# Expert outputs sent one by one to DRAM, with accumulating DMAs, in a fused retention and mixture-of-experts kernel

## The chip, the cores and the metric

The kernel runs on one core of a Trainium2 chip. A core has a matrix engine (TensorE, PE in the profile, with its weight loads as PEld), a vector engine (VectorE, DVE), a scalar engine (ScalarE, ACT), GpSimd (POOL) and SyncE (SP), which issues most DMAs. The metric is the device time of one execution in microseconds (us), the median of several runs. Less is better.

## The reference

The first stage is a causal retention over 8 batches, 8 heads, 576 positions and 64 values per head. The second is a mixture of 4 experts, whose outputs are weighted by normalised probabilities and summed:

```python
scores = scale * np.matmul(q, k.transpose(0, 1, 3, 2))
Dmat = np.where(rel >= 0, gamma[:, None, None] ** rel[None, :, :], 0.0)
attn = np.matmul(scores * Dmat[None], v)              # 8 x 8 x 576 x 64
x = attn.transpose(0, 2, 1, 3).reshape(4608, 512)
p = domain_probs / (domain_probs.sum(-1, keepdims=True) + 1e-09)
for e in range(4):                                    # w1[e] 512 x 1024, w2[e] 1024 x 512
    h = np.maximum(x @ w1[e], 0.0)
    out += p[:, e:e + 1] * (h @ w2[e])                # out 4608 x 512, float32
```

## The kernel before

The 4608 tokens are cut into 9 tiles of 512 (`nt` 0 to 8), and a tile into 4 subtiles of 128 tokens. A stage is one tile and one expert. All weights stay in SBUF as bf16.

Tile 0 and the up projection of tile 1's expert 0 are done in a head with ordinary matmuls, while attention of the batches 0 and 1 runs. After it come the stages from tile 1, expert 1 on. In each, `up_fast` computes the up projection of the stage with one level of a Strassen-like scheme (seven products for eight) in two halves, g = 0 and g = 1. Between its products it calls `fill(1)` to `fill(4)`, which put matmuls of the previous stage's down projection in between, so that TensorE has work while the other engines move results. From a certain stage on for each expert the down projection uses the scheme too (class `Down`, one object per half, with banks V and W in PSUM): half `s` of a stage yields the subtiles `s` and `s + 2`. For tile 1's experts 0 and 3 and tile 2's expert 0, as for tile 0, it is the ordinary one (`downs`, which yields the subtiles 0 to 3 in order).

The work of attention for the batches 2 to 7 stands in queues of one class (`Chain`), one queue per engine. Every call of `between`, `window` and `sums` takes the next piece whose needs were emitted before. The order of the instructions on each engine is thus fixed when the program is built, and each engine runs its own in order.

Rows of the program that the steps below touch:

- L684: VectorE adds P and m5 into bank R (`upR`). The next product of TensorE into P waits until it has read P.
- L692 and L693: VectorE adds, then GpSimd applies the ReLU to that quarter of hT.
- L593, L595, L597, L599: VectorE makes the sums of hT that the next `Down` needs. L593 of half 1 stands between the two outputs (`last_sum`).
- L569 to L572: VectorE makes the token sums of the next tile, when a tile begins.
- L650, L652, L654: `Down.out`. For expert 0, VectorE scales the output from V (L652) and ScalarE the one from W (L650) into `acc`. For experts 1 to 3, VectorE does both as one fused scale and add on `acc` (L654).
- L529 and L531: the same for the ordinary path, scaled by ScalarE for expert 0 and added by VectorE for the others.
- L657 and L534: after expert 3, SP sends the finished subtile of 256 KB to DRAM.
- L333 and L339 to L340: the masks of attention on VectorE, and on ScalarE with an affine select on GpSimd. L242: ScalarE copies attention's output into the tile of tokens. L279 to L291: GpSimd casts raw loads. L366 and L369: running sums of attention's state. L297 and L299: SP issues DMA transposes. L111 to L133: SP issues the raw loads, each when a cast has set a raw buffer free. L420: the casts of batch 0 on VectorE and GpSimd. L148 and L153: GpSimd issues the weight loads, which cast float32 to bf16.
- L672 and L623: the matmuls of the up and of the down projection.

The accumulators lie in SBUF: four buffers of 128 x 512 float32, one for each subtile of a tile, kept over the tile's four experts.

Of the kernel before, what the change touches and what calls it, by code (L numbers as in the profile page):

```python
# [9 lines left out]
FP32 = mybir.dt.float32  # L10
# [4 lines left out]
MULT = mybir.AluOpType.mult  # L15
ADD = mybir.AluOpType.add
# [7 lines left out]
def kernel(  # L24
# [10 lines left out]
    nc = tc.nc  # L35
    B, H, S, D = q.shape
    N, E = moe_domain_probs.shape
    _, Dm, F = moe_w1.shape
# [8 lines left out]
    NFC = F // 128  # L47
    NT = 512
    n_nt = N // NT
    NSUB = NT // 128  # L50
# [8 lines left out]
    att1 = ctx.enter_context(tc.tile_pool(name="att1", bufs=1))  # L59
    att2 = ctx.enter_context(tc.tile_pool(name="att2", bufs=2))  # L60
    hpool = ctx.enter_context(tc.tile_pool(name="hpool", bufs=2))
    apool = ctx.enter_context(tc.tile_pool(name="apool", bufs=NSUB))
    xpool = ctx.enter_context(tc.tile_pool(name="xpool", bufs=3))
    tpool = ctx.enter_context(tc.tile_pool(name="tpool", bufs=1))
    psum = ctx.enter_context(tc.tile_pool(name="psum", bufs=1, space=PSUM))
# [6 lines left out]
    def bank(ring, shape, dtype, name):  # L72
        tag = RINGS[ring][turn[ring] % len(RINGS[ring])]
        turn[ring] += 1
        return psum.tile(shape, dtype, tag=tag, name=name)
# [4 lines left out]
    def after(ins, dep):  # L80
        tc.add_manual_dep(ins.ins, dep.ins.name,
                          mybir.DependencyInfo(mybir.DependencyClass.Sync, mybir.DependencyReason.DATA),
                          reason="start order")
# [58 lines left out]
    w1_sb, w2_sb = [], []  # L142
# [71 lines left out]
    probs = const.tile([128, E, NTT], FP32)  # L214
# [36 lines left out]
    class Att:  # L251


        def __init__(self, b):
            self.b, self.t = b, state[b]
            self.m, self.qkT, self.sT, self.s = {}, {}, {}, {}
# [235 lines left out]
                put_x(nc.vector, slice(2 * u, 2 * u + 2), self.b * S + 256 * hf + c * C, os[c])  # L492


    acc, hTs, tsum, ssum, dsum, hsum = {}, {}, {}, {}, {}, {}

    def up_classical(nt, e, lead=0, cut=NT // 2, pause=False):
# [21 lines left out]
    def downs(nt, e, ring):  # L519

        hT = hTs[nt, e]
        if e == 0:
            acc[nt] = [apool.tile([128, Dm], FP32, tag="acc", name="acc") for _ in range(NSUB)]

        def evacuate(po, ns, cols):
            t = nt * NSUB + ns
            pe, a = probs[:, e, t:t + 1], acc[nt][ns][:, cols]
            if e == 0:
                nc.scalar.activation(a, po, Copy, scale=pe)  # L529
            else:  # L530
                nc.vector.scalar_tensor_tensor(a, po, pe, a, op0=MULT, op1=ADD)  # L531
            if e == E - 1:
                eng = nc.scalar if cols.start else nc.sync
                eng.dma_start(out=out[t * 128:(t + 1) * 128, cols], in_=a)  # L534

        for ns in range(NSUB):
            w = Dm // 2 if (nt, ns, e) == (n_nt - 1, NSUB - 1, E - 1) else Dm
            for d in range(0, Dm, w):
                po = bank(ring, [128, w], FP32, "po")
                for fc in range(NFC):  # L540
                    nc.tensor.matmul(po, lhsT=hT[:, fc, ns * 128:(ns + 1) * 128],  # L541
                                     rhs=w2_sb[e][:, fc, d:d + w], start=(fc == 0), stop=(fc == NFC - 1))
                    yield None if fc < NFC - 1 else lambda: evacuate(po, ns, slice(d, d + w))

    def down_groups(nt, e):
        for f in downs(nt, e, "mm"):
            if f:
                f()
                yield
# [51 lines left out]
    class Down:  # L601
# [2 lines left out]

        def __init__(self, nt, e, s, tags=("o0", "o1")):
            self.nt, self.e, self.s, self.tags = nt, e, s, tags
            if e == 0 and s == 0:
                acc[nt] = [apool.tile([128, Dm], FP32, tag="acc", name="acc") for _ in range(NSUB)]

        def product(self, i, part=slice(0, NFC // 2)):  # L610
            hT, h, w, t = hTs[self.nt, self.e], hsum[self.nt, self.e], w2_sb[self.e], dsum[self.e]
# [28 lines left out]
            nc.vector.tensor_tensor(o, i, x, op=ADD)  # L640

        def out(self, i, halves=(slice(0, 2),)):
            ns = 2 * i + self.s
            t, po = self.nt * NSUB + ns, (self.V, self.W)[i]
            pe = probs[:, self.e, t:t + 1]
            for x in halves:
                cols = slice(x.start * HD, x.stop * HD)
                a, src = acc[self.nt][ns][:, cols], po[:, x].rearrange("p a d -> p (a d)")
                if self.e == 0 and i == 1:
                    nc.scalar.activation(a, src, Copy, scale=pe)  # L650
                elif self.e == 0:
                    nc.vector.tensor_scalar_mul(a, src, pe)  # L652
                else:
                    nc.vector.scalar_tensor_tensor(a, src, pe, a, op0=MULT, op1=ADD)  # L654
                if self.e == E - 1:
                    eng = nc.scalar if len(halves) == 1 and x.start else nc.sync
                    eng.dma_start(out=out[t * 128:(t + 1) * 128, cols], in_=a)  # L657

    def up_fast(nt, e, g, fill, window, sums):

# [334 lines left out]
    for nt, e in [(nt, e) for nt in range(1, n_nt) for e in range(E)][1:]:  # L995
        fast = before >= begin[before[1]]
        fill_classical = None if fast else downs(*before, "po")
        while pay(nt, e, late=True):
            pass
# [142 lines left out]
```

## Time and profile before

| what | value |
|---|---|
| median of 3 runs | 521.08 us (520.82 to 521.61) |
| the profiled execution's own time | 521.82 us |
| its span, first to last instruction | 520.1 us |
| HBM read, written | 45.16 MB, 9.44 MB |
| output DMAs | 32 of 256 KB and 8 of 128 KB, all issued by SP |
| VectorE, L654 | 88 of 512 columns, 0.749 us (from V) and 0.742 us (from W) |
| ScalarE, L650 | 12, 0.689 us |
| VectorE, L652 | 12, 0.751 us |

The profile is of one execution. "Busy" is the time in which an engine executes; a row of the timeline has the start, the length, engine, line, operation, the tiles written and read, and, in brackets, how long the engine was idle before it and what released it. Releasers are inferred from semaphores. A matmul's start tells more than its end, which is modelled.

### The profile page before, as it was taken

Reading aid. Unit: us, or ns where it says so; the run is one execution under the profiler, and the core shown is the slowest. Engines: PE = TensorE matmul, PEld = TensorE weight load, DVE = VectorE, ACT = ScalarE, POOL = GpSimd, SP = SyncE. Lnnn points to the kernel's source line nnn. Section 1 sums busy time; section 2 is a strip of 40 time slices with the busy share of each in tenths; the row PEclk is TensorE's granted clock in tenths of the full one; section 3 lists DMA queues with packets and bytes.
Section 4 is the critical chain, followed back from the end, with each engine's and each line's share of the span. In section 5 each row is a group of like instructions: output and inputs, shape, how many; then the busy total and the mean of one; then the engine's idle time right before and its main releaser. Section 6 shows DMA issues by size and latency. Waiting matters only on the chain.

```text
span 520.1 us, 12551 instructions
## 1 busy us (share of the span) xinstructions
PE 505.5 (97%) x4871; PEld 401.6 (77%) x4886; DVE 388.8 (75%) x720; ACT 308.7 (59%) x637; POOL 196.1 (38%) x299
## 2 busy tenths in 40 slices
PE   8999999999999999999999999999999999999995
PEld 3644455678667878888888888888888888888884
DVE  6624579877646888779877987887788878787776
ACT  3462264666446756666666666766666667666661
POOL 6702275644433444444443543354345310000010
PEclk9999999999999999999999999999999999999999
DMA  9999998926183145525463538433941020011002
GB/s 239 187 208 201 199 204 184 160 48 113 42 203 62 42 101 134 137 57 114 95 159 72 112 70 196 72 89 65 204 95 42 13 80 2 2 41 42 2 1 82
DMA packets 149836, 54.24 MB, mean 104 GB/s; under 512 B 131308, under 2 KB 144620, under 8 KB 149776
## 3 DMA queue, kind: packets, MB, share of 16 engines
q1 hardware_dynamic: 142448, 45.05, 40.1%
q0 software_dynamic: 7328, 8.39, 9.5%
q8 instruction: 38, 0.62, 0.5%
q14 instruction: 22, 0.18, 0.1%
HBM read 45.16 MB, written 9.44 MB: 105 GB/s over the span
## 4 chain that ended last, share of the span: by engine, by line
PE 89%; DVE 7%; issue 2%; DMA 1%; ACT 0%; DVEq 0%; SPq 0%
PE upP L672 20%; PE downV L623 18%; PE downW L623 13%; PE upR L672 10%; PE po L541 8%; PE ph L500 6%; PE upQ L672 5%; PE s L328 2%; DVE acc L654 1%; PE oc L379 1%; PE kvp L346 1%; DVE upR L684 1%; PE oc L376 1%; DMA raw<-in_q_dram 1%; DVE sT L333 1%
## 5 line engine op out<-in xcount | busy, mean ns | idle before, releaser
L672 PEld LDWEIGHTS <-wt 128*128 128x128 bf16 x992 | 94.9, 98 | 18.0 <-issue 3.8
L623 PEld LDWEIGHTS <-hT 128*128 128x128 bf16 x928 | 90.8, 98 | 11.1 <-issue 0.6
L693 POOL TENSOR_SCALAR hT<-hT 128x512 bf16<-128x512 bf16 x62 | 38.3, 618 | 160.5 <-DVE hT L692 160.4
L672 PEld LDWEIGHTS <-wsum 128*128 128x128 bf16 x744 | 72.7, 98 | 12.2 <-issue 2.6
L623 PE MATMUL downV<-wt,hT 128*128 128x256 bf16 x464 | 78.4, 273 | 0.4 <-DVE acc L654 0.4
L672 PE MATMUL upP<-xT,wt 128*128 128x256 bf16 x496 | 74.4, 272 | 2.1 <-DVE upR L684 1.7
L623 PEld LDWEIGHTS <-hsum 128*128 128x128 bf16 x696 | 67.8, 98 | 8.7 <-DVE hsum L593 0.3
L684 DVE TENSOR_TENSOR upR<-upP,m 128x512 f32<-128x512 f32 x62 | 43.1, 696 | 35.8 <-PE upP L672 22.1
L700 ACT ACTIVATE hT<-upP 128x512 bf16<-128x512 f32 x62 | 37.0, 597 | 53.0 <-PE upP L672 39.2
L695 ACT ACTIVATE hT<-upR 128x512 bf16<-128x512 f32 x62 | 37.0, 597 | 32.7 <-PE upR L672 32.6
L541 PE MATMUL po<-wt,hT 128*128 128x512 bf16 x214 | 52.1, 379 | 0.6
L678 ACT ACTIVATE upQ<-upP 128x512 f32<-128x512 f32 x62 | 36.3, 586 | 26.0 <-PE upP L672 25.9
L340 POOL TENSOR_SCALAR_AFFINE_SELECT sT<-sT 128x512 bf16<-128x512 bf16 x24 | 15.2, 634 | 96.1 <-ACT sT L339 80.4
L654 DVE SCALAR_TENSOR_TENSOR acc<-downV,probs,acc 128x512 f32<-128x512 f32 (+1 forms) x48 | 34.6, 726 | 22.5 <-PE downV L623 22.4
L686 ACT ACTIVATE hT<-upQ 128x512 bf16<-128x512 f32 x62 | 37.0, 597 | 22.3 <-PE upQ L672 22.3
L692 DVE TENSOR_TENSOR hT<-upP,m 128x512 bf16<-128x512 f32 x62 | 42.8, 690 | 6.5 <-PE upP L672 4.7
L516 ACT ACTIVATE hT<-ph 128x512 bf16<-128x512 f32 x40 | 23.5, 597 | 29.1 <-PE ph L500 28.2
L672 PE MATMUL upR<-tsum,wsum 128*128 128x256 bf16 x248 | 37.2, 272 | 2.3 <-DVE tsum L569 2.3
L680 ACT ACTIVATE m<-upR 128x512 f32<-128x512 f32 x62 | 36.8, 594 | 2.2 <-PE upR L672 2.2
L672 PE MATMUL upP<-tsum,wt 128*128 128x256 bf16 x248 | 37.3, 273 | 0.1
L672 PE MATMUL upP<-tsum,wsum 128*128 128x256 bf16 x248 | 37.2, 273 | 0.0
L672 PE MATMUL upR<-xT,wsum 128*128 128x256 bf16 x248 | 37.2, 273 | 0.0
(136 smaller groups left out, 974.2 us busy)
## 6 DMA issues: line engine op xcount, KB each, us to landing
out_dram<-acc SPq DMA_DIRECT2D x32, 256.0 KB, 2.9
wt<-in_moe_w_dram POOLq DMA_DIRECT2D x6, 1024.0 KB, 26.2
raw_k<-in_k_dram SPq DMA_DIRECT2D x24, 256.0 KB, 3.3
raw_q<-in_q_dram SPq DMA_DIRECT2D x24, 256.0 KB, 3.6
raw_v<-in_v_dram SPq DMA_DIRECT2D x24, 256.0 KB, 3.8
raw<-in_k_dram SPq DMA_DIRECT2D x8, 256.0 KB, 5.6
raw<-in_q_dram SPq DMA_DIRECT2D x8, 256.0 KB, 5.8
raw<-in_v_dram SPq DMA_DIRECT2D x8, 256.0 KB, 5.5
```

The source lines that it names most:

```text
L541: nc.tensor.matmul(po, lhsT=hT[:, fc, ns * 128:(ns + 1) * 128], rhs=w2_sb[e][:, fc, d:d + w], start=(fc == 0), stop=(fc == NFC - 1))
L623: nc.tensor.matmul(o, lhsT=l[:, k, self.s * 128:(self.s + 1) * 128], rhs=r[:, k], start=(i == 1 and k == 0), stop=(k == NFC // 2 - 1), ski ...
L654: nc.vector.scalar_tensor_tensor(a, src, pe, a, op0=MULT, op1=ADD)
L672: nc.tensor.matmul(ps[:, l], lhsT=wa(kc)[:, f:f + 128], rhs=xa(kc), start=(start and l == 0 and kc == 0), stop=(kc == 1), skip_group_check ...
L678: nc.scalar.activation(Q, P, Copy)
L680: nc.scalar.activation(m5, R_, Copy)
L684: nc.vector.tensor_tensor(R_, P, m5, op=ADD)
L686: nc.scalar.activation(hT[:, lo, t0], Q, Relu)
L692: nc.vector.tensor_tensor(h22, P, m5, op=ADD)
L693: nc.gpsimd.tensor_scalar(h22, h22, float("inf"), 0.0, op0=MIN, op1=MAX)
L695: nc.scalar.activation(hT[:, lo, t1], R_, Relu)
L700: nc.scalar.activation(hT[:, hi, t0], P, Relu)
```

## The change

In tiles 1 to 7 nothing is accumulated in SBUF any more. Each expert's output is scaled by its probability into a buffer of two subtiles: the first of a pair by VectorE and the second by ScalarE on the path of `Down`, both by ScalarE on the ordinary path. Then the pair (512 KB) is sent. For expert 0, SP sends it as a plain write. For experts 1 to 3, GpSimd issues a DMA that adds to what is in DRAM. Such a DMA waits for the landing of those that wrote the same rows for the expert before. The pairs are (s, s + 2) on the path of `Down`, and (0, 1) and (2, 3) on the ordinary one. Tiles 0 and 8 go on adding in SBUF and are sent after expert 3. The buffers are two of 128 x 2 x 512 in place of four of 128 x 512. The ordinary path loses its splitting of the very last output in two halves.

```diff
-    apool = ctx.enter_context(tc.tile_pool(name="apool", bufs=NSUB))
+    apool = ctx.enter_context(tc.tile_pool(name="apool", bufs=2))
...
+    out_rows = out.rearrange("(x p) d -> p x d", p=128)
+    sent = {}
+
+    def on_chip(nt):
+        return nt in (0, n_nt - 1)
+
+    def out_pair(nt, e, pair, j):
+
+        if e == 0 or not on_chip(nt):
+            acc[nt, j] = apool.tile([128, 2, Dm], FP32, tag="acc", name="acc")
+        return acc[nt, j]
+
+    def send(nt, e, pair, j):
+        x = slice(nt * NSUB + pair[0], nt * NSUB + pair[1] + 1, pair[1] - pair[0])
+        if e == 0:
+            i = nc.sync.dma_start(out=out_rows[:, x, :], in_=acc[nt, j])
+        else:
+            i = nc.gpsimd.dma_start(out=out_rows[:, x, :], in_=acc[nt, j], accum_op=ADD)
+            for p, d in sent[nt, e - 1]:
+                if set(p) & set(pair):
+                    after(i, d)
+        sent.setdefault((nt, e), []).append((pair, i))
...
     def downs(nt, e, ring):
...
-        if e == 0:
-            acc[nt] = [apool.tile([128, Dm], FP32, tag="acc", name="acc") for _ in range(NSUB)]
-
-        def evacuate(po, ns, cols):
-            t = nt * NSUB + ns
-            pe, a = probs[:, e, t:t + 1], acc[nt][ns][:, cols]
-            if e == 0:
+        def evacuate(po, ns):
+            t, pair, j = nt * NSUB + ns, (ns // 2 * 2, ns // 2 * 2 + 1), ns // 2
+            a = (acc[nt, j] if ns % 2 else out_pair(nt, e, pair, j))[:, ns % 2]
+            pe = probs[:, e, t:t + 1]
+            if e == 0 or not on_chip(nt):
                 nc.scalar.activation(a, po, Copy, scale=pe)
             else:
                 nc.vector.scalar_tensor_tensor(a, po, pe, a, op0=MULT, op1=ADD)
-            if e == E - 1:
-                eng = nc.scalar if cols.start else nc.sync
-                eng.dma_start(out=out[t * 128:(t + 1) * 128, cols], in_=a)
+            if not on_chip(nt):
+                if ns % 2:
+                    send(nt, e, pair, j)
+            elif e == E - 1:
+                nc.sync.dma_start(out=out[t * 128:(t + 1) * 128, :], in_=a)
...
         def out(self, i, halves=(slice(0, 2),)):
-            ns = 2 * i + self.s
-            t, po = self.nt * NSUB + ns, (self.V, self.W)[i]
-            pe = probs[:, self.e, t:t + 1]
+            nt, e, j, pair = self.nt, self.e, self.s, (self.s, self.s + 2)
+            if i == 0:
+                out_pair(nt, e, pair, j)
+            t, po, acc_ = nt * NSUB + pair[i], (self.V, self.W)[i], acc[nt, j][:, i]
+            pe = probs[:, e, t:t + 1]
             for x in halves:
                 cols = slice(x.start * HD, x.stop * HD)
-                a, src = acc[self.nt][ns][:, cols], po[:, x].rearrange("p a d -> p (a d)")
-                if self.e == 0 and i == 1:
+                a, src = acc_[:, cols], po[:, x].rearrange("p a d -> p (a d)")
+                if e and on_chip(nt):
+                    nc.vector.scalar_tensor_tensor(a, src, pe, a, op0=MULT, op1=ADD)
+                elif i == 1:
                     nc.scalar.activation(a, src, Copy, scale=pe)
-                elif self.e == 0:
+                else:
                     nc.vector.tensor_scalar_mul(a, src, pe)
-                else:
-                    nc.vector.scalar_tensor_tensor(a, src, pe, a, op0=MULT, op1=ADD)
-                if self.e == E - 1:
+                if e == E - 1 and on_chip(nt):
                     eng = nc.scalar if len(halves) == 1 and x.start else nc.sync
                     eng.dma_start(out=out[t * 128:(t + 1) * 128, cols], in_=a)
+            if i == 1 and not on_chip(nt):
+                send(nt, e, pair, j)
```

More of the change, by code (lines that the diff above doesn't have):

```diff
@@ L531, in evacuate @@
                 nc.vector.scalar_tensor_tensor(a, po, pe, a, op0=MULT, op1=ADD)
-            if e == E - 1:
-                eng = nc.scalar if cols.start else nc.sync
-                eng.dma_start(out=out[t * 128:(t + 1) * 128, cols], in_=a)
-        for ns in range(NSUB):
[L537 to L543, printed above, removed]
+            if not on_chip(nt):
[3 more added lines that the diff above has]
+                nc.sync.dma_start(out=out[t * 128:(t + 1) * 128, :], in_=a)
+        for ns in range(NSUB):
+            po = bank(ring, [128, Dm], FP32, "po")
+            for fc in range(NFC):
+                nc.tensor.matmul(po, lhsT=hT[:, fc, ns * 128:(ns + 1) * 128],
+                                 rhs=w2_sb[e][:, fc, :], start=(fc == 0), stop=(fc == NFC - 1))
+                yield None if fc < NFC - 1 else lambda: evacuate(po, ns)
     def down_groups(nt, e):
@@ L606, in __init__ @@
             self.nt, self.e, self.s, self.tags = nt, e, s, tags
-            if e == 0 and s == 0:
-                acc[nt] = [apool.tile([128, Dm], FP32, tag="acc", name="acc") for _ in range(NSUB)]
         def product(self, i, part=slice(0, NFC // 2)):
```

## The prediction

> **What bounds the kernel now.** I read the page's busy times, then the stretches of the span, then the waits of TensorE, and last the timeline around those waits. First the busy times:
>
> ```profile
> span 520.1 us, 12551 instructions
> PE 505.5 (97%) x4871; PEld 401.6 (77%) x4886; DVE 388.8 (75%) x720; ACT 308.7 (59%) x637; POOL 196.1 (38%) x299
> ```
>
> A share over the whole span hides where the 3% lies, so the stretches (columns: length, then busy us and count of PE, PEld, DVE, ACT, POOL, the clock, the DMA share, GB/s):
>
> ```profile
> 92.00:135.00 43.00, 41.23 (x406) 32.51 (x407) 33.17 (x57) 26.46 (x54) 21.41 (x30) 1.00 0.52 93
> 245.00:299.40 54.40, 53.91 (x570) 46.79 (x569) 44.33 (x83) 35.84 (x76) 24.24 (x39) 1.00 0.50 109
> 408.00:457.00 49.00, 49.00 (x473) 43.75 (x471) 39.17 (x75) 32.85 (x70) 6.67 (x13) 1.00 0.06 23
> ```
>
> From 408 us on TensorE has no gap at all; a faster VectorE can give nothing there. While attention of the next batches runs between the matmuls (92 to 408 us) TensorE has small gaps, with VectorE at 81% (44.33 of 54.40). So the gain is capped by these gaps. To size them I took the starts of the matmuls in the timeline: those of 256 columns lie 109 ns apart, and each longer step is a slip. Slips at the switch to attention's smaller matmuls (about 0.31 us each) stay. The slips from 92 us on that end on VectorE are, by time: 94.8 (1.31 us), 116.2 (0.33), 129.9 (0.20), 134.4 (1.12), 190.7 (1.46), 207.3 (0.21), 249.0 (0.25), 261.4 (0.56), 303.4 (0.25), 315.9 (0.21), 369.7 (0.21), five of 0.04 to 0.09 (0.31 together), 379 and 382 (0.35), 493.7 (0.21). The waits of TensorE name the releasers:
>
> ```profile
> PE upR L672 <- DVE tsum L569: 2.3, 2, 1.3
> PE upP L672 <- DVE upR L684: 1.7, 3, 1.1
> ```
>
> How such a slip comes about is seen on VectorE in the timeline from 257.9 us (start, length, line, tiles, idle before):
>
> ```profile
> 257.92 0.75 DVE L654 SCALAR_TENSOR_TENSOR acc<-downV,probs,acc 128x512 f32<-128x512 f32 x1 [0.44 <-PE downV L623]
> 258.58 0.71 DVE L593 TENSOR_TENSOR hsum<-hT 128x512 bf16<-128x512 bf16 x1
> 259.22 0.74 DVE L654 SCALAR_TENSOR_TENSOR acc<-downW,probs,acc 128x512 f32<-128x512 f32 x1
> 259.88 0.41 DVE L595 TENSOR_TENSOR hsum<-hsum,hT 128x512 bf16<-128x512 bf16 x1
> 260.74 0.69 DVE L599 TENSOR_TENSOR hsum<-hT,hsum 128x1024 bf16<-128x1024 bf16 x1 [0.46 <-ACT downW L629]
> 261.35 0.69 DVE L684 TENSOR_TENSOR upR<-upP,m 128x512 f32<-128x512 f32 x1
> ```
>
> upR (L684) stands at the end of an in-order row of work that begins with the two outputs, and TensorE's next product into bank P waits for it. From the start of the first output to that of upR pass 3.43 us here; 3.08, 3.09 and 3.09 in the halves of the 0.21 slips; 2.97 where the slip is 0.09; 2.69 where there is none. The second output (L654 from downW) costs this row 0.66 us, start to start.
>
> **The change part by part.** *VectorE loses work.* In tiles 1 to 7, experts 1 to 3, the Strassen path has 40 halves; each sheds one L654 from downW: 40 × 0.742 = 29.7 us. The classical path of tile 1's expert 3 sheds 4 × 0.749 (L531) = 3.0. The first output stays: a scale costs 0.751 (L652), the fused scale and add 0.749. VectorE: 388.8 − 32.7 = 356 us busy. This counts only where the row above ends in a slip. The two tile starts (134.4, 190.7) have L569 straight behind the second output: 0.66 each, 1.32. The slips of 116.2, 207.3, 249.0, 303.4, 315.9, 369.7 and the five small ones have an unbroken row from the outputs to upR, and each is shorter than 0.66: 0.33 + 0.21 + 0.25 + 0.25 + 0.21 + 0.21 + 0.31 = 1.77. At 261.4, L599 has an idle 0.46 whose end another engine may set, so between 0 and 0.56; half, 0.28. Not touched: 94.8 (its outputs belong to tile 1's expert 0), 129.9 (VectorE was idle 1.60 before it), what is left of the tile starts, 379 and 382, tile 8. Sum: 1.32 + 1.77 + 0.28 = 3.4 us off.
>
> *ScalarE gains it.* 40 × 0.689 (L650) + 4 × 0.688 (L529) = 30.3 us: 308.7 becomes 339. Expert 0 of tiles 3 to 8 already runs this way, so the trace shows such halves, one in the most crowded place, behind a copy of attention's output:
>
> ```profile
> 211.34 0.59 ACT L242 ACTIVATE xT<-oc 128x512 bf16<-128x512 f32 x1
> 211.81 0.69 ACT L650 ACTIVATE acc<-downW,probs 128x512 f32<-128x512 f32 x1
> 212.38 0.61 ACT L678 ACTIVATE upQ<-upP 128x512 f32<-128x512 f32 x1
> ```
>
> Its first output starts at 211.28 and upR at 213.97: 2.69 us, the same as in the uncrowded half at 433.79 to 436.48. No slip follows. So I put ScalarE at nothing; its cover is 0.19 us (slips appear from an offset of 2.88).
>
> *GpSimd issues 42 accumulating DMAs* (7 tiles × 3 experts × 2 pairs). None is in the trace. The nearest rows are its weight loads: 0.78 us at L148 (1 MB), 0.91 at L153. I take 0.8: 34 us, 196 becomes 230. Each stands behind both outputs, at about 434.92 in the late half, and the next GpSimd work there is the ReLU of hT (L693) at 438.89; so 4.0 us are free for it. In attention's halves the casts stand ahead of it in the queue, and the affine select behind it starts only 4 us later (215.89 after outputs at 211). Behind a send that is stuck stand L693 and behind that L593 on VectorE, which TensorE waits for.
>
> Here the Trainium skill speaks against the change. "SBUF — State Buffer", section "SBUF: two separate sides", has VectorE and GpSimd share one pair of ports under an exclusive lock, and a VectorE instruction with two SBUF inputs is held by a GpSimd one that reads SBUF. The trace agrees for casts: L593 takes 0.71 above beside a cast, against 0.42 alone. If a send held the port likewise, 20 of the 40 halves (those with L595, L599 right behind the outputs) would lose about 0.29, less the slack: up to 5.8 us, and the gain would be gone. The row for a DMA issue speaks otherwise:
>
> ```profile
> 15.37 1.48 POOL L148 DMA_DIRECT2D wt<-in_moe_w_dram  x2
> 15.50 0.68 DVE L420 TENSOR_TENSOR qm<-raw,gq 128x512 bf16<-128x512 f32 x1
> ```
>
> Both inputs of L420 lie in SBUF, and inside two DMA issues it took 0.68, its shortest (0.79 and more elsewhere). I count nothing.
>
> *The DMA engines.* Plain output costs 5.9% of 16 engines over 105 us for 2.23 MB (400 to 505 us): 22.5 GB/s per engine, 1.46 us of all 16 for 512 KB. For an accumulation the near row is the weight load, which reads two bytes for each one that it writes:
>
> ```profile
> q0 software_dynamic: 7328, 8.39, 9.5%
> ```
>
> 9.5% × 520.1 × 16 = 790 us for 8.39 MB written: 10.6 GB/s per engine. "Collectives: The Full Stack", section "The bandwidth ceiling: the fold count and why AG ≠ RS ≠ AR", says that an adding transfer runs at half the rate of a copy since it reads two sources; by that 2 × 1.46 = 2.9 us per 512 KB, by the row 524 KB / (16 × 10.6) = 3.1. I take 3.1, between 1.5 (the add is free) and 6. Per tile of 54.4 us: loads 0.50 × 54.4 = 27.2, less the old output of 2.9, plus 2 × 1.46 + 6 × 3.1 = 21.5: 45.8 us, 84%. Full at (54.4 − 24.3 − 2.9) / 6 = 4.5 us each. A send has one stage of 12.2 us to land before its buffer is needed and the next send on its rows waits for it; the plain 256 KB took 2.1 us to land at the end and 2.9 in the median, so about 1.4 + 3.1 alone and 8 beside loads. Loads that lie behind a send come perhaps 3 us later; after 100 us the trace has raw_k and raw_q landing 3.4 us or more before their cast, and transposes 3.3 us or more before their matmuls. This cover is thin, so I set 0.4 us against the gain.
>
> *SP and the buffers.* SP sheds 28 issues of 256 KB and gets 14 of 512 KB; nothing waited for its outputs. The two pair buffers hold what four tiles held. Both cost nothing. Cutting the last tile's w from the classical path does nothing: tile 8 takes the other path.
>
> Sum: −3.4 + 0.4 = −3.0 us. The profiled execution took 521.82 us for its span of 520.1, 0.7 above the median of the runs, 521.08; the difference is taken from the median: 518.1.
>
> **The rivals.** *VectorE's time does not reach TensorE* (521.0, no change): the waits named above are inferred, and once VectorE is earlier, ScalarE or an unexplained wait like the 0.46 may end the same slips. For it: 408 us onward shows TensorE full with any split. Against: the unbroken rows. Gain 0 to 1 us.
> *Accumulations too slow* (slower): if one takes over 4.5 us of the engines, or 12.2 us to land, the next send on its rows holds GpSimd, L693 stands behind it, and VectorE waits for the buffer. At 5.5 us each a tile needs 24.3 + 2.9 + 33 = 60.2 us of DMA instead of 54.4; over four full tiles with loads about +23 us, 544; just past the point, +2 us, 523. The DMA share of 0.50 speaks for it, the 3.1 against.
> *A GpSimd issue over 4.0 us* has the same end through L693 alone; the rows of 0.8 speak against it.
>
> **How the numbers follow.** Gain as summed 0.64; no reach 0.18; slow accumulations or issues 0.18. A difference under 0.2% (1.0 us) can't be told from none. Low end: all VectorE slips after 110 us but tile 8's, some 5.3 us, would give 515.8; with part of it 516.4. High end: 523, just past the saturation point; the 544 lies outside, with about half of the slower case. The likeliest case's own range is 516.4 to 519.8.
>
> **What would show it.** In the profile after: DVE near 356, ACT near 339, POOL near 230 us; the PE waits on L569 halved; stretches after 408 us unchanged (12.2 us per stage); accumulations landing in 4 to 8 us; no L693 wait on a DMA. Wrong if POOL's waits show out_dram, if sends take over 4 us on POOL, or if L593 and L599 grow beside them.

## The result and the profile after

The changed kernel took 518.02 us in the median of 4 runs (517.26 to 518.86), against 521.29 us before (4 runs); the ratio is 0.9938, with a 95% interval from 0.9921 to 0.9956. Two more series on chip time of their own gave 0.9964 (0.9949 to 0.9978) and 0.9950 (0.9936 to 0.9964). So the gain lies between 1.9 and 3.3 us. The profiled execution took 517.96 us.

The lines moved: L650 is now L675, L652 is L677, L684 is L709, L593 is L616, L595, L599 are L618, L622, L629 is L650, L693 is L718, L569 is L592, L570 is L593; the accumulating send is L514. First, of the page of the kernel after, the span, the engines, the software DMA queue and the two kinds of sends:

```profile
span 516.2 us, 12668 instructions
PE 502.8 (97%) x4886; PEld 400.8 (78%) x4886; DVE 365.2 (71%) x676; ACT 333.2 (65%) x681; POOL 248.0 (48%) x341
q0 software_dynamic: 18752, 30.41, 36.8%
L514 POOL DMA_DIRECT2D out_dram<-acc x42 | 51.3, 1221 | 31.8 <-ACT acc L675 22.4
out_dram<-acc POOLq DMA_DIRECT2D x42, 512.0 KB, 6.3
out_dram<-acc SPq DMA_DIRECT2D x14, 512.0 KB, 3.7
```

VectorE has shed work and ScalarE and GpSimd have taken some. A send holds GpSimd for 1.22 us and lands after 6.3 us in the median. Then the same three stretches as in the prediction (the same columns):

```profile
92.00:135.00 43.00, 41.86 (x409) 33.28 (x410) 32.25 (x56) 28.86 (x57) 25.69 (x34) 1.00 0.89 159
245.00:299.40 54.40, 54.40 (x578) 47.61 (x577) 42.12 (x79) 39.72 (x84) 32.23 (x45) 1.00 0.98 171
408.00:457.00 49.00, 49.00 (x473) 43.75 (x471) 35.63 (x70) 35.57 (x73) 14.31 (x19) 1.00 0.49 86
```

From 245 us TensorE now has no gap, while the DMA share went from 0.50 to 0.98. The last stretch is as long as before. Of TensorE's waits, the two shown of the kernel before (here L592 and L709) and one that is new:

```profile
PE s L328 <- DMA qkT<-km: 1.0, 2, 0.6
PE upR L697 <- DVE tsum L592: 1.0, 2, 0.6
PE upP L697 <- DVE upR L709: 0.8, 2, 0.6
```

The waits on VectorE have halved, and two on a DMA transpose have come in. VectorE's row of work that was shown from 257.9 us is here, one output shorter:

```profile
254.97 0.75 DVE L677 TENSOR_SCALAR acc<-downV,probs 128x512 f32<-128x512 f32 x1 [0.44 <-PE downV L644]
255.64 0.72 DVE L616 TENSOR_TENSOR hsum<-hT 128x512 bf16<-128x512 bf16 x1
256.39 0.42 DVE L618 TENSOR_TENSOR hsum<-hsum,hT 128x512 bf16<-128x512 bf16 x1
256.92 0.69 DVE L622 TENSOR_TENSOR hsum<-hT,hsum 128x1024 bf16<-128x1024 bf16 x1
257.66 0.70 DVE L709 TENSOR_TENSOR upR<-upP,m 128x512 f32<-128x512 f32 x1
```

From the first output to upR pass 2.69 us instead of 3.43: the value that the prediction had from a half without a slip. The idle 0.46 us ahead of L599 (here L622) has gone too.

**A ledger of the time.** TensorE loads the same weights in the same order in all kernels here (4886 loads, and 6 records of its sequencer), so two executions can be laid on each other load by load, and each step of the difference has a place. Before to after, from 114 us on:

| place (us, before) | step (us) | what stands there |
|---|---|---|
| 130 | -0.20 | upR |
| 136, 192 | -0.63, -0.70 | token sums at a tile start |
| 208, 249, 262, 304, 316, 370 | -0.21, -0.32, -0.56, -0.32, -0.21, -0.30 | upR behind the outputs |
| 379, 382, 494 | -0.19, -0.16, -0.30 | other rows of VectorE |
| 209, 372 | +0.69, +0.46 | attention's S waits for a DMA transpose |
| after the last matmul | +0.63 | the last outputs and their landing |

The gains sum to 4.1 us, the costs to 1.8; together -2.3. The other 1.6 us of the 3.9 between the two spans lie before 114 us. The table below, from one profiled execution each, therefore counts from the 900th of these records (at 112 to 114 us) to the end:

| kernel | 900th load at | from there to the end | median, ratio to before |
|---|---|---|---|
| before | 114.2 | 405.9 | 1 |
| after (three executions) | 112.6, 114.4, 114.2 | 403.6, 403.7, 405.6 | 0.9938, 0.9964, 0.9950 |
| second output on VectorE | 114.0 | 407.5 | 523.58, 1.0061 |
| no accumulating sends | 113.2 | 402.7 | 517.82, 0.9943 |
| narrow sends | 111.9 | 402.6 | 516.53, 0.9917 |
| before, less the second output | 113.9 | 402.3 | 517.79, 0.9939 |
| more bytes | 113.9 | 412.2 | 526.85, 1.0110 |
| transposes first, everywhere | 112.7 | 403.0 | 517.86, 0.9946 |
| transposes first, four pieces | 112.4, 112.7 | 402.5, 402.5 | 517.29, 0.9937 and 517.00, 0.9930 |

Five of the steps have a common mark. In the kernel before, VectorE stands idle for 0.46 us ahead of the instructions at 260.7, 377.8 and 493.0 us, and the late upR of the slip at 129.9 us starts after an idle 1.60 us where the version with the second output back on VectorE (described below) has 1.22. In the trace, semaphore waits counted, these instructions are VectorE's records 448, 704, 960 and 192: exactly 256 apart. The profile names a different releaser each time, and for the last one only VectorE itself, which had been done. That one, then the same place in the version named:

```profile
492.98 0.42 DVE L595 TENSOR_TENSOR hsum<-hsum,hT 128x512 bf16<-128x512 bf16 x1 [0.46 <-DVE hsum L593]
```

```profile
493.51 0.42 DVE L618 TENSOR_TENSOR hsum<-hsum,hT 128x512 bf16<-128x512 bf16 x1
```

The slips at 129.9, 261.4, 379, 382 and 493.7 us stand behind these pauses, and none is left at these places in any other kernel here, whether its row is shorter or not. They are 1.4 us of the 4.1. What makes VectorE pause is not shown, and there is one profile of the kernel before.

### The profile page after: what moved, and what is told of

The parts are those of the page before. It is cut to its first block, busy times and chain, and to the rows that moved or that the text cites. A ratio compares the mean times of both kernels' runs of the same rounds, so it can differ in the third digit from the quotient of the medians.

```text
span 516.2 us, 12668 instructions
## 1 busy us (share of the span) xinstructions
PE 502.8 (97%) x4886; PEld 400.8 (78%) x4886; DVE 365.2 (71%) x676; ACT 333.2 (65%) x681; POOL 248.0 (48%) x341
## 3 DMA queue, kind: packets, MB, share of 16 engines
q0 software_dynamic: 18752, 30.41, 36.8%
## 4 chain that ended last, share of the span: by engine, by line
PE 90%; DMA 4%; DVE 4%; issue 1%; SPq 0%; DVEq 0%
PE upP L697 20%; PE downV L644 18%; PE downW L644 13%; PE upR L697 10%; PE po L564 9%; PE ph L525 7%; PE upQ L697 5%; DMA qkT<-km 3%; PE s L328 2%; PE oc L379 1%; PE oc L376 1%; PE kvp L346 1%; DMA raw<-in_q_dram 1%; DVE sT L469 1%; DVE acc L673 1%
## 5 line engine op out<-in xcount | busy, mean ns | idle before, releaser
L718 POOL TENSOR_SCALAR hT<-hT 128x512 bf16<-128x512 bf16 x62 | 38.0, 613 | 108.5 <-DVE hT L717 108.4
L709 DVE TENSOR_TENSOR upR<-upP,m 128x512 f32<-128x512 f32 x62 | 43.3, 698 | 53.3 <-ACT downW L650 38.2
L514 POOL DMA_DIRECT2D out_dram<-acc x42 | 51.3, 1221 | 31.8 <-ACT acc L675 22.4
L677 DVE TENSOR_SCALAR acc<-downV,probs 128x512 f32<-128x512 f32 x52 | 38.9, 749 | 28.6 <-PE downV L644 28.2
L564 PE MATMUL po<-wt,hT 128*128 128x512 bf16 x224 | 53.4, 379 | 0.0
L675 ACT ACTIVATE acc<-downW,probs 128x512 f32<-128x512 f32 x52 | 35.9, 690 | 8.3 <-PE downW L644 8.3
```

The costliest lines, as they stand in the source:

```text
L514: i = nc.gpsimd.dma_start(out=out_rows[:, x, :], in_=acc[nt, j], accum_op=ADD)
L709: nc.vector.tensor_tensor(R_, P, m5, op=ADD)
L718: nc.gpsimd.tensor_scalar(h22, h22, float("inf"), 0.0, op0=MIN, op1=MAX)
```

## The experiments

Theory A: the gain is VectorE's shorter row from the outputs to upR, and the accumulating DMAs only make that possible, at a price. A whole series compares with the kernel before on its own chip; versions from different chips compare by these ratios and by the ledger.

**The changed kernel beside the next three.**

> The changed kernel itself, on the same chip as the three runs beside it. Both theories expect 518.0 us, within 0.6, and 3.3 us less than the kernel before.

Measured: 518.78 us, 520.81 before; ratio 0.9964 (0.9949 to 0.9978). The gain is 2.0 us, less than the 3.3 expected. From the 900th load on its execution took 403.7 us, as the first one (403.6); it differs in the head.

**The second output back on VectorE, the sends kept.**

```diff
-                elif i == 1:
+                elif i == 1 and e == 0:
                     nc.scalar.activation(a, src, Copy, scale=pe)
```

> The changed kernel, with the second output of experts 1 to 3 scaled by VectorE and not by ScalarE; the sends are as in the changed kernel. Theory A (the gain is VectorE's row of work from the outputs to upR being 0.66 us shorter): the slips of TensorE at 207, 249, 262, 303, 316, 370 us and at the two tile starts come back, together 3.2 us; 521.2 us, between 520.5 and 522. Rival B (the gain comes from something else that the change did: fewer issues on SP, no reading of the accumulators, an earlier head): it stays at 518.0, at most 518.6.

Measured: 523.58 us, ratio 1.0061 (1.0039 to 1.0083): slower than the kernel before. Against the changed kernel the ledger has 0.63 and 0.71 back at the tile starts and 0.22, 0.34, 0.23, 0.33, 0.22, 0.32 at the others, 3.0 us together. The 0.23 is a new slip, at 257 us there; the 0.56 of 261.4 us stays away, and so do the four other slips behind a pause. From the first output to upR pass 2.86 us there (257.80 to 260.66) with the second output in the row and no pause, and no slip follows. Its row of VectorE at the second of these tile starts (190 us):

```profile
189.77 0.75 DVE L677 TENSOR_SCALAR acc<-downV,probs 128x512 f32<-128x512 f32 x1 [1.00 <-PE downV L644]
190.44 0.41 DVE L616 TENSOR_TENSOR hsum<-hT 128x512 bf16<-128x512 bf16 x1
190.77 0.74 DVE L677 TENSOR_SCALAR acc<-downW,probs 128x512 f32<-128x512 f32 x1
191.44 0.41 DVE L592 TENSOR_TENSOR tsum<-xT 128x512 bf16<-128x512 bf16 x1
```

The token sum stands 0.67 us behind the start of the second output, and TensorE's wait for it is back at 2.2 us in two waits (2.3 before). So theory A holds for about 2.7 us of the gain, and rival B falls for these; the 1.4 us behind the pauses stay off though the second output is back. The time was 1.6 us above the range of theory A. Later transposes are 0.6 of that (1.77 us here at two places, 1.15 in the changed kernel's first profile), and the changed kernel itself was 0.8 slower on this chip than in its first series; the rest is not explained. The sends without the relief are a loss.

**No accumulating sends.**

```diff
         if e == 0:
             i = nc.sync.dma_start(out=out_rows[:, x, :], in_=acc[nt, j])
+        elif e:
+            return
```

> The changed kernel with the accumulating DMAs left out: the outputs of experts 1 to 3 in tiles 1 to 7 are computed and scaled but go nowhere, so the output lacks them. Theory A with a price for the DMAs (two slips of TensorE on a DMA transpose that lands late, 0.69 and 0.46 us, are caused by the accumulating DMAs): 516.9 us, between 516.3 and 517.3. Rival C (the DMAs cost nothing on the path, the late transposes would come anyway): 518.0.

Measured: 517.82 us, ratio 0.9943 (0.9928 to 0.9957), 1.0 us below the changed kernel on that chip. The number alone missed theory A's range (516.3 to 517.3) and lay near rival C's 518.0, as both started from 518.0 for the changed kernel, which took 518.78 here. The ledger decides: just two steps over 0.2 us stand after 114 us, -0.62 and -0.46, at the two places of the late transposes. Rival C falls.

**Narrow sends.**

```diff
-            i = nc.gpsimd.dma_start(out=out_rows[:, x, :], in_=acc[nt, j], accum_op=ADD)
+            i = nc.gpsimd.dma_start(out=out_rows[:, x, 0:16], in_=acc[nt, j][:, :, 0:16], accum_op=ADD)
```

> The changed kernel with accumulating DMAs of 16 of 512 columns: GpSimd issues 42 of them as before and they wait for one another, but they move 16 KB and not 512 KB, so the output lacks the rest of the sum. Theory A (the bytes on the DMA engines make the transposes late): the slips of 0.69 and 0.46 us go, 0.9 to 1.2 us less than the changed kernel, as without the sends; ratio to the kernel before about 0.994. Rival D (GpSimd's issue of 1.22 us and its waits delay the casts and so the transposes): no gain over the changed kernel.

Measured: 516.53 us, ratio 0.9917 (0.9903 to 0.9932). GpSimd is as busy as in the changed kernel (248.4 us), and its waits stay, but both slips go (-0.68, -0.44). So the bytes make the transposes late, and GpSimd's 51 us cost nothing after 114 us: rival D falls. The changed kernel had no series on this chip. The landing of the transposes, narrow sends first, then the changed kernel (count, median us from issue to landing):

```profile
qkT<-qm SPq DMA_TRANSPOSE x24, 3.5
qkT<-km SPq DMA_TRANSPOSE x24, 2.7
```

```profile
qkT<-qm SPq DMA_TRANSPOSE x24, 6.1
qkT<-km SPq DMA_TRANSPOSE x24, 4.1
```

Its median is 1.3 us under that without sends, from another chip, although the two agree from the 900th load on (402.6 and 402.7). That part lies in the first 112 us, where the two hardly differ, and stays unexplained.

**The kernel before, less the second output.**

```diff
-                if self.e == 0 and i == 1:
+                if i == 1 and self.e and self.nt not in (0, n_nt - 1):
+                    pass
+                elif self.e == 0 and i == 1:
```

> The kernel before, with the second output of experts 1 to 3 in tiles 1 to 7 not added at all on the path of Down (VectorE sheds 40 instructions, ScalarE gains none, nothing is sent that was not before); the output lacks those addends. Theory A (VectorE's shorter row is the gain, ScalarE's extra 30 us cost nothing): the same slips go as in the changed kernel, 3.2 to 3.5 us less than the kernel before, within 0.4 us of the changed kernel without its sends. Rival E (ScalarE's work eats part of the gain): this one is 1 us or more below the changed kernel without its sends.

Measured: 517.79 us, ratio 0.9939 (0.9923 to 0.9956): 3.3 us off with nothing else touched. The ledger has the same steps as the changed kernel (0.63, 0.70, 0.21, 0.31, 0.56, 0.32, 0.21, 0.29). The pauses have moved here too: the slips at 129.9, 379, 382 and 493.7 us are gone, and a new one of 0.21 at 465 us stands behind an idle 0.45 ahead of L595. So this run takes the row and the pauses together, and only the run with the second output put back tells them apart. Without the 0.65 us after the last matmul, which only the kernels built on the changed one have, the version without sends takes 402.0 us from the 900th load and this one 402.3 (two chips). ScalarE's work cost nothing that shows: rival E falls.

**More bytes.**

```diff
             i = nc.gpsimd.dma_start(out=out_rows[:, x, :], in_=acc[nt, j], accum_op=ADD)
+            nc.sync.dma_start(out=spare[next(spares)], in_=acc[nt, j])
```

> The changed kernel with each pair of experts 1 to 3 also written, plainly and by SP, to a spare tensor in DRAM: 512 KB more for each accumulating DMA. By the sum in the prediction, with 3.3 us for an accumulation as the profile after has it, a tile of 54.4 us then needs 24.3 + 2.9 + 6 x (3.3 + 1.46) = 55.8 us of the DMA engines. Theory A (the rival of slow accumulations decides near that point): TensorE waits for transposes and GpSimd for landings, 3 to 12 us more than the changed kernel. Rival F (the point is further off since transfers of two queues overlap): under 2 us more.

Measured: 526.85 us, ratio 1.0110 (1.0085 to 1.0135), some 8.5 us above the changed kernel. The stretch from 245 us, three waits of TensorE and one of VectorE:

```profile
245.00:299.40 54.40, 51.65 (x552) 44.99 (x550) 39.58 (x75) 37.53 (x78) 30.28 (x43) 1.00 1.13 216
```

```profile
PE downV L647 <- DVE acc L680: 4.1, 2, 2.8
PE upP L700 <- ACT hT L728: 1.9, 1, 1.9
PE s L328 <- DMA qkT<-km: 1.8, 2, 1.4
DVE acc L680 <- DMA spare<-acc: 7.9, 4, 3.1
```

The longest wait of TensorE is for VectorE's first output (here L680), which itself needs a pair buffer that the extra write has not yet read (the last line, of VectorE's waits). GpSimd waited for the landing of a send just once, 0.7 us. So of the slower rival's chain one part shows, the late buffer, and it was brought about by plain writes. With a share of 0.98 TensorE ran without a gap; 8.8 us more of DMA work per tile cost some 2 us per tile. As the extra writes hold the same buffers and SP's queue, this does not tell a full set of engines from late buffers, and a slower accumulation itself was not tried.

**Transposes ahead of the raw load.** The order on SP after the cast of a q piece was: raw load, then the two transposes. First turned round everywhere:

```diff
             def cast(f, *args, then=None):
                 f(*args)
+                if then:
+                    then()
                 loads["cast"] += 1
                 load_ahead(len(PIECES))
...
-                add("POOL", lambda c=c: (cast(A.cast, "q", c, g), transposes(c)))
+                add("POOL", lambda c=c: cast(A.cast, "q", c, g, then=lambda: transposes(c)))
```

> The changed kernel with one order turned round on SP: after the cast of a q piece the two DMA transposes are issued ahead of the raw load that the cast sets free, not behind it. Theory A2 (the late transposes stand behind that load in the hardware queue and beside an accumulating DMA): the two slips of 0.69 and 0.46 us go, 516.9 us, between 516.5 and 517.4. Rival (the accumulating DMA alone makes them late, the order does not matter): 518.0, at least 517.6.

Measured: 517.86 us, ratio 0.9946 (0.9928 to 0.9964), 0.9 us below the changed kernel on that chip. The number missed theory A2's range (up to 517.4) and lay in that of its rival, again with 518.0 as the base of both; the ledger decides for A2. The two slips go (-0.70, -0.46), and a new one of 0.41 us comes at 172.8 us (the expectation below has it as 0.29). GpSimd there:

```profile
171.28 1.23 POOL L514 DMA_DIRECT2D out_dram<-acc  x1 [3.92 <-ACT u L654]
172.57 0.63 POOL L340 TENSOR_SCALAR_AFFINE_SELECT sT<-sT 128x512 bf16<-128x512 bf16 x1
```

The send started 3.92 us after GpSimd's last work and the affine select stood behind it, for which TensorE waited. In the changed kernel the send starts at 169.4 us. It waits for the landing of expert 0's plain send: that one lands at 168.84 us in the changed kernel and at 170.72 here, and in both the next send starts 0.56 us behind it. SP now issues the plain send right behind a raw load, where the two transposes stood between them; that this makes it land late was argued from SP's order, and then used: the same turn only for the first piece of the batches 4 to 7, where the two late transposes stand.

```diff
+                if c == 0 and b >= 4:
+                    add("POOL", lambda c=c: cast(A.cast, "q", c, g, then=lambda: transposes(c)))
+                else:
+                    add("POOL", lambda c=c: (cast(A.cast, "q", c, g), transposes(c)))
```

> The changed kernel with the transposes ahead of the raw load only for the first piece of the batches 4 to 7, where the two late ones were; elsewhere the order is that of the changed kernel, so that the send of expert 0 of tile 2, behind which GpSimd's next send waited with the order turned round everywhere, comes as early as before. Theory: both slips on transposes go and the new one of 0.29 us at 172.8 us does not come: 1.1 us less than the changed kernel, 0.2 to 0.3 less than with the order turned round everywhere. Rival: no better than that one.

Measured: 517.29 us, ratio 0.9937 (0.9920 to 0.9953). Both slips go (-0.62, -0.44) and the new one does not come; from the 900th load 402.5 us against 403.0. The medians, from two chips, can't tell the two versions apart. It was run again beside the changed kernel:

> The changed kernel beside the version with the transposes ahead for the first pieces, on one chip. Both theories expect 2 to 3.3 us less than the kernel before.

> The version with the transposes ahead of the raw load for the first pieces of the batches 4 to 7, beside the changed kernel. If the two slips on late transposes (1.1 us together) are all that it mends: 0.8 to 1.3 us less than the changed kernel. If the scatter from the first 90 us hides it: a difference under 0.5.

Measured: the changed kernel 518.67 us (22 runs, 516.82 to 521.58), ratio 0.9950 (0.9936 to 0.9964); the version with the transposes ahead 517.00 us (14 runs), ratio 0.9930 (0.9911 to 0.9949). It is 1.7 us lower in the median, more than the 1.1 that it mended in the first profile; the intervals overlap a little. The profiled execution of the changed kernel was here its longest, 521.58 us, and shows why the price varies. TensorE at the same two places:

```profile
209.18 0.40 PE L328 MATMUL s<-qkT 64*128 64x128 bf16 x8 [1.61 <-DMA qkT<-km]
...
371.29 0.40 PE L328 MATMUL s<-qkT 64*128 64x128 bf16 x8 [1.38 <-DMA qkT<-km]
```

The same two transposes land so late that TensorE stands 3.0 us, where the first execution lost 1.0. With the transposes ahead, TensorE's waits have no line for them. Among the versions with a complete output this one has the lowest median.

## Why the prediction was right, point by point

**VectorE's row sets the gain.** Right for the larger part. Putting the second output back (+4.8 us in all) returns 2.7 us of slips at their old places; taking it away alone gives -3.3 us, with the pauses moved as well. The tile starts were put at 0.66 each and gave 0.63 and 0.70. The slips at 207, 249, 303, 316 and 370 us went whole. At 261.4 half of 0.56 was counted and all of it went. The prediction's own offsets would have had it go whole (3.43 less 0.66 is 2.77, below 2.88); but with the second output put back it stayed away too, as the idle 0.46 was gone. So that slip needed both, the second output and the pause, and no other engine had set its end.

**The slip at 116.2 us (0.33) was counted as gone and stayed.** What failed is the step that every unbroken row gets shorter by 0.66. The freed time was taken back in the same row. VectorE in the kernel after, at that place:

```profile
111.22 0.74 DVE L677 TENSOR_SCALAR acc<-downV,probs 128x512 f32<-128x512 f32 x1
111.87 1.55 DVE L593 TENSOR_TENSOR dsum<-wt,dsum 128x1024 bf16<-128x1024 bf16 x1
```

and GpSimd:

```profile
111.83 1.04 POOL L279 TENSOR_TENSOR qm<-raw_q,gq 128x512 bf16<-128x512 f32 x1
```

Before, that sum of two SBUF tiles (dsum) started two thirds of a microsecond later against the cast and took 0.89 us. Now it starts just behind the start of a GpSimd cast that reads SBUF, and takes 1.55. In both it ends 0.55 us behind the end of that cast (113.42 and 112.87 us; before 115.00 and 114.45), so the cast sets the end of the row. The sum takes 1.55 in each of the kernels without the second output in the row, whether they send or not, and 0.89 with the second output put back on VectorE. This fits the exclusive lock that the prediction took from the Trainium skill, "SBUF — State Buffer", section "SBUF: two separate sides"; it was weighed for the sends alone and not for the casts that a shorter row would meet.

**Not touched, and gone all the same:** 129.9, 379, 382 and 493.7 us, 0.85 together. These are the slips behind VectorE's pauses, and no term of the prediction held them. That they went is luck of where the pauses fall in the new program. Gains counted 3.4, measured 4.1: the rows 2.7, the places behind pauses 1.4.

**ScalarE at nothing:** right, by the version without sends and the kernel before less the second output.

**A send does not hold the port:** right. In the row shown from 254.97 us, L618 and L622 keep 0.42 and 0.69 us, and L622 lies inside this issue on GpSimd:

```profile
256.68 1.25 POOL L514 DMA_DIRECT2D out_dram<-acc  x1 [0.61 <-ACT upQ L703]
```

**GpSimd's issue** was put at 0.8 us and took 1.22; the 4.0 us that were free covered it. POOL came to 248 us, not 230.

**The DMA engines.** An accumulation was put at 3.1 us of 16 engines. From the page: 36.8% of 516.2 us less 9.5% of 520.1 us is 140.6 us, over 42 it is 3.35; the six after 432 us, beside almost nothing, come to 3.6. The doubling taken from the Trainium skill, "Collectives: The Full Stack", section "The bandwidth ceiling: the fold count and why AG ≠ RS ≠ AR" (an estimate of 2.9; the page states it for the reduce step of a collective), was low, the row of the weight loads nearer. Landing with no loads beside it was put at 4.5 and took 5.7 (the sends after 432 us). All sends of this profile landed within 9.0 us, under the 12.2 that they have.

**The late transposes** were put at 0.4 us, as a thin cover; this term was mis-sized: 1.15 and 1.1 us in the first two profiles of the changed kernel, 3.0 in the third. The transposes do have a thin cover. What the prediction left out is what stands ahead of them in SP's own order: turning one load round them gave the price back.

**After the last matmul** all kernels built on the changed one but that with more bytes take 6.3 us to the end, those built on the one before 5.6. The prediction had the two buffers at nothing. SP's third output DMA starts 0.37 us later there, behind VectorE's fourth add. That two subtiles now share a tile is not enough to cause it: the version with more bytes shares them too and starts that DMA as early as the kernel before. The cause is open.

**The sum** was -3.0 and the time forecast 518.1. The terms measured from 114 us on give -2.3: 0.7 more gain than counted, by the pauses, and 1.4 more cost, by the transposes and the end. That these errors partly cancel is luck, and so is that the first series came nearer still to the forecast: that part is the scatter of the first 114 us. (For the low end, the slips listed behind 110 us sum to 5.5, not 5.3; nothing rests on it.) DVE was put at 356 us and came to 365.2, ACT at 339 and came to 333.2: neighbouring instructions overlap by some 0.08 us in the profile, so one taken out of a row, or put into one, changes the busy time by less than its length. VectorE's lengths fell by 30.3 us in sum (some other sums grew), its busy time by 23.6.

## What to carry to other kernels

When TensorE is 97% busy, list its gaps by place and ask for each which in-order row ends last there; the 0.7 us that an instruction takes is worth what these gaps hold, here some 3 us of the 30 that VectorE shed. A slip that goes may have had another cause than the one in view: putting the removed instruction back tells which slips were its own. A row that gets shorter meets other neighbours: see what its instructions will lie beside. And when bytes move from an engine to the DMA queues, look at the transfers with the thinnest cover and at what is issued just ahead of them on the same queue.

## What the runs showed of the hardware

- An accumulating DMA of 512 KB from SBUF to DRAM cost 3.35 us of the 16 engines, against 1.46 for a plain one of that size, landed after 5.7 us alone, and held GpSimd 1.22 us, with 16 columns as with 512.
- A DMA share of 0.98 over 54 us left TensorE without a gap. The share, summed over the packets of the queues, can pass 1 (1.13 with more bytes), so 1.0 is no hard end.
- VectorE paused for 0.46 us ahead of records 256 apart in the kernel before (260.7, 377.8 and 493.0 us). A changed number of instructions moved the pauses, and 1.4 us of slips went with them.
- The part up to the 900th load took the changed kernel 112.6, 114.4 and 114.2 us in three executions, with the DMA engines full in most of it. A difference of 1 us in the whole time says little of a change later on; the part behind that load repeated within 0.1 us in the two profiles of the version with four pieces' transposes ahead.
